# Linear and memory attention on one core: diagonal blocks of two query tiles packed into shared exponentials

## The chip, the cores and the metric

The kernel runs on one core of one Trainium2 chip. The time is the device time of one execution in microseconds; the runs of the kernel before gave 514.81, 516.71 and 517.5 us, median 516.71. A profiled execution is a run of its own, with a time of its own.

## What is computed

Two layers A (softmax attention in segments, with a memory) and two layers B (linear attention with learned features), in the order A, B, A, B, each with LayerNorm ahead and a residual. 2048 tokens, width 512, 32 heads of 16.

```python
# A, for each segment s of 512 tokens
logits = einsum('bhqd,bhkd->bhqk', qs, ks) * scale + mask     # causal inside the segment
a_dot = einsum('bhqk,bhkd->bhqd', softmax(logits), vs)
pq = phi(qs)                                   # phi(t) = t + 1 for t > 0, else exp(t)
a_mem = (pq @ M) / (pq @ z + 1e-06)            # state of the segments before
o = g * a_mem + (1.0 - g) * a_dot              # g = sigmoid(beta)
M = M + phi(ks)^T @ vs;  z = z + sum(phi(ks))
# B
phi_q = concat(softmax(q @ w_phi), softmax(-q @ w_phi));  phi_k likewise from k
o = (phi_q @ (phi_k^T @ v)) / (phi_q @ sum(phi_k) + 1e-06)
# around both: x = x + f(layernorm(x)) @ wo
```

## The kernel before

The residual stream X stays in SBUF for the whole run, 16 tiles of 128 tokens (a tile's tokens on the partitions, in order). A segment is 4 tiles. "Layer" below is one A with the B behind it; there are two.

**Order of the work.** Nothing is issued in program order. Each call to `P.add` records an operation with its reads, writes, a cost and the engines that may run it; `schedule` then simulates the engines with these costs and writes out one queue for each engine, in which the order is fixed. Among the operations that could start, the one with the lowest priority number goes first; the numbers are the tuple PLAN (L44, 3455 entries, one for each operation in order of recording; L296). An operation with two possible engines (`copy`, L784: ACT or DVE) is put where it starts first. A wait on the chip is a wait on semaphores of the operations that it depends on. Two strips of score matmuls that lie in different row groups are written out in turn, two matmuls of the one, two of the other (L689 to L695). Where PE would be idle, matmuls on zeros (L1450) are put in.

**A, segment by segment.** `ln` (L999): statistics on DVE, the power -0.5 on POOL, the normalised tile `xn` on DVE, transposed to `xnT` by DMA (SP's queue) or by PE for the tiles in `by_pe`. `a_proj` (L1057): for the keys either one token-major projection, split into even and odd heads and transposed by DMA, or, for tiles in `by_pe`, a feature-major projection with two masked evictions (L1076) *and* a token-major one (L1085) for phi. `by_pe` is all four tiles of segment 0 of both layers, and nothing else. `phi` (L1025): exponential on ACT, minimum with 1 on DVE, then max(t, 0) plus that on DVE. Then queries (QT), PhiQ, and V.

`a_att` (L1152) is the softmax attention of a group of query tiles ts; groups are (0, 1) and (2, 3) for segments 0 to 2, and (0, 1), (2), (3) for segment 3 (L1392). For every key tile j and parity of heads there is a strip part of 128 columns for each query tile i >= j, for four groups g of 8 heads. Four parts fill 512 columns; two banks of PSUM (two heads) make a tile `st` of 128 x 1024, written by row-tiled matmuls of 32 contraction rows. One ACT exponential of 1024 (L1199) evicts it to PT (12 buffers). A diagonal part (i = j) is computed in full, 128 keys by 128 queries, and its upper half is set to zero afterwards by POOL (L1203). With P transposed, `PT` is the stationary operand of the PV matmuls (17 columns: 16 values and the gated normaliser). DVE takes the reciprocal of the sums (L1222) and multiplies, one tile at a time (L1224); the memory part AM is added per tile (L1233). `a_out` (L1243) projects and adds to X on DVE (L1241).

**B.** `b_keys` (L1251): two exponentials a tile on ACT (L1261), sums (L1262) and reciprocals (L1264) on DVE, the scaling of 128 x 1024 on POOL (L1266; on DVE for the last two tiles of segment 3). `b_queries` (L1300) and `b_out` (L1337) follow when the keys of all four segments are in KV; the output goes out with `store` in layer 1. The B outputs of layer 0 lie mostly beside layer 1's attention; chunk 0 of them stands between the layers, since segment 0 of layer 1 needs it.

Of the kernel before, what the change touches and what calls it, by code (L numbers as in the profile page):

```python
# [26 lines left out]
ENGS = ("pe", "act", "dve", "pool", "sp")  # L27
HOP = dict(pe=0.03, act=0.03, dve=0.03, pool=0.05, sp=0.04)
# [11 lines left out]
OVERLAP = 0.14  # L40
PRI = dict(mem=-5.0, state=0.5, aout=-0.2, lnx0=-0.5, lnx1=-10.0, ap0=9.5, aps=4.625, bo0=-6.0, bo1=3.5, lnb=-7.5, bk=2.0, bks=2.2, kv=14.0, q00=58.0,
# [140 lines left out]
)  # L182


# [1311 lines left out]
```

## Time and profile before

| | |
|---|---|
| median of three runs | 516.71 us |
| profiled execution | 518.92 us |
| its span, first to last instruction | 517.3 us |
| granted PE clock, mean | 0.987 |
| busy: PE, ACT, DVE, POOL | 487.7, 440.3, 432.3, 269.8 us |
| exponentials of scores (L1199) | 320, 1054 ns each, 308.2 us busy |
| selections on diagonals (L1203) | 168 of 512, 80 of 256, 32 of 768 elements; 660, 419, 886 ns |
| normalising multiplies (L1224) | 128 of 128 elements, 281 ns |
| score matmuls | 832 of 256 columns, 896 of 128 |
| PV matmuls | 2560 of 17 columns |
| matmuls on zeros (L1450) | 125, 19.7 us |

In rows of the profile an engine, a line, what is written and read, the shape and the count come first, then busy time and mean length of one, then the idle time ahead of them and what ended it. Busy times overlap where an engine works on two instructions at once, so the distance from one start to the next is often shorter than the length of one. PEld is PE's loading of weights.

### The profile page before, as it was taken

Reading aid. Unit: us, or ns where it says so; the run is one execution under the profiler, and the core shown is the slowest. Engines: PE = TensorE matmul, PEld = TensorE weight load, DVE = VectorE, ACT = ScalarE, POOL = GpSimd, SP = SyncE. Lnnn points to the kernel's source line nnn. Section 1 sums busy time; section 2 is a strip of 40 time slices with the busy share of each in tenths; the row PEclk is TensorE's granted clock in tenths of the full one; section 3 lists DMA queues with packets and bytes.
Section 4 is the critical chain, followed back from the end, with each engine's and each line's share of the span. In section 5 each row is a group of like instructions: output and inputs, shape, how many; then the busy total and the mean of one; then the engine's idle time right before and its main releaser. Section 6 shows DMA issues by size and latency. Waiting matters only on the chain.

```text
span 517.3 us, 16946 instructions
## 1 busy us (share of the span) xinstructions
PE 487.7 (94%) x7194; PEld 306.4 (59%) x7286; DVE 432.3 (84%) x1025; ACT 440.3 (85%) x593; POOL 269.8 (52%) x396
## 2 busy tenths in 40 slices
PE   9989999999999999999999999999999999999997
PEld 6656455656456656656665555655555555565664
DVE  6998789968669888899968788988998677887995
ACT  3989999989999999854599999899999999974443
POOL 5464486635567766230147468456854476631234
PEclk9989999989999999999999999999999999997999
DMA  8956433332200411200115425224433121110034
GB/s 240 272 93 94 79 67 53 38 57 46 49 13 15 59 39 22 26 4 5 22 22 74 55 39 94 54 41 64 63 63 63 23 55 33 13 37 4 4 82 142
DMA packets 94538, 29.96 MB, mean 58 GB/s; under 512 B 86272, under 2 KB 94464, under 8 KB 94464
## 3 DMA queue, kind: packets, MB, share of 16 engines
q1 hardware_dynamic: 93216, 27.83, 30.0%
q10 hardware_dynamic: 1248, 1.06, 0.8%
q8 instruction: 57, 0.93, 0.8%
q14 instruction: 17, 0.14, 0.1%
HBM read 6.32 MB, written 2.10 MB: 16 GB/s over the span
## 4 chain that ended last, share of the span: by engine, by line
PE 52%; ACT 32%; DVE 11%; DMA 2%; issue 2%
PE PS L729 48%; ACT PT L1199 25%; PE PS L1450 3%; DMA xnT<-xn 2%; ACT Ek L1261 2%; ACT phi L1027 2%; DVE stats L1007 1%; PE PS L807 1%; DVE X L1241 1%; DVE O L1358 1%; DVE KV L1293 1%; DVE EQ L1332 1%; DVE Rkv L1295 1%; DVE rd L1357 0%; DVE PhiK L1029 0%
## 5 line engine op out<-in xcount | busy, mean ns | idle before, releaser
L1199 ACT ACTIVATE PT<-PS 128x1024 bf16<-128x1024 f32 x320 | 308.2, 1054 | 10.0 <-PE PS L729 9.1
L1203 POOL TENSOR_SCALAR_AFFINE_SELECT PT<-PT 128x512 bf16<-128x512 bf16 (+2 forms) x280 | 169.7, 617 | 131.7 <-ACT PT L1199 128.0
L729 PEld LDWEIGHTS PS<-VT,PT 128*128 128x128 bf16 x2560 | 78.1, 96 | 23.3 <-issue 5.8
L729 PE MATMUL PS<-VT,PT 128*128 128x17 bf16 x2560 | 85.7, 171 | 0.1
L729 PE MATMUL PS<-QT,KT 32*128 32x256 bf16 (+1 forms) x864 | 77.4, 245 | 4.5 <-ACT PT L1199 2.9
L1266 POOL TENSOR_TENSOR Ek<-Ek,rZ 128x1024 bf16<-128x1024 bf16 x28 | 55.3, 1977 | 44.7 <-DVE rZ L1264 44.7
L729 PE MATMUL PS<-QT,KTo 32*128 32x128 bf16 (+1 forms) x864 | 76.1, 243 | 2.4 <-ACT PT L1199 1.0
L729 PEld LDWEIGHTS PS<-QT,KT 32*128 32x128 bf16 x864 | 32.4, 92 | 39.2 <-ACT PT L1199 24.0
L1261 ACT ACTIVATE Ek<-PS 128x512 bf16<-128x512 f32 x64 | 35.8, 611 | 13.1 <-PE PS L729 12.8
L729 PEld LDWEIGHTS PS<-QT,KTo 32*128 32x128 bf16 x864 | 35.0, 93 | 19.6 <-ACT PT L1199 11.6
L1241 DVE TENSOR_TENSOR X<-X,PS 128x512 bf16<-128x512 bf16 x54 | 36.8, 682 | 11.3 <-PE PS L729 10.7
L1262 DVE TENSOR_REDUCE Zk<-Ek 128x64 f32<-128x1024 bf16 x32 | 38.6, 1212 | 8.2 <-ACT Ek L1261 7.9
L1007 DVE BATCH_NORM_STATS2 stats<-X 128x6 f32<-128x512 bf16 x64 | 43.3, 683 | 1.5 <-DMA X<-in_A_x_dram 0.8
L1013 POOL TENSOR_TENSOR rstd<-rstd,negh 128x2 f32<-128x2 f32 (+1 forms) x38 | 26.3, 694 | 33.3 <-DVE rstd L1011 32.1
L729 PE MATMUL PS<-xnT,WA_q 128*128 128x128 bf16 x512 | 35.9, 221 | 0.1
L729 PE MATMUL PS<-WA_v,xnT 128*128 128x512 bf16 x110 | 31.9, 380 | 2.4 <-issue 1.0
L729 PE MATMUL PS<-WA_k,xnT 128*128 128x512 bf16 x111 | 31.4, 380 | 2.8 <-issue 1.0
L729 PEld LDWEIGHTS PS<-xnT,WA_q 128*128 128x128 bf16 x512 | 29.6, 99 | 7.0 <-issue 2.8
L1224 DVE TENSOR_TENSOR O<-PS,r 128x128 bf16<-128x128 f32 x128 | 31.5, 281 | 1.2
L729 PE MATMUL PS<-WA_o,OT 128*128 128x512 bf16 x115 | 30.0, 380 | 1.4 <-issue 0.6
L729 PE MATMUL PS<-WB_o,OT 128*128 128x512 bf16 x118 | 29.6, 380 | 1.4 <-DVE QT L785 0.5
L1017 DVE TENSOR_SCALAR xn<-X,mv,rstd 128x512 bf16<-128x512 bf16 x64 | 26.9, 430 | 2.0 <-DMA xnT<-xn 0.9
(135 smaller groups left out, 839.1 us busy)
## 6 DMA issues: line engine op xcount, KB each, us to landing
out_dram<-X SPq DMA_DIRECT2D x16, 128.0 KB, 1.8
X<-in_A_x_dram SPq DMA_DIRECT2D x3, 512.0 KB, 10.0
EQ<-in_B_wqkv_dram SPq DMA_DIRECT2D x2, 512.0 KB, 10.5
OT<-O SPq DMA_TRANSPOSE x46, 2.5
xnT<-xn SPq DMA_TRANSPOSE x36, 2.5
WA_o<-in_A_wo_dram SPq DMA_DIRECT2D x1, 512.0 KB, 10.1
WB_v<-in_B_wqkv_dram SPq DMA_DIRECT2D x1, 512.0 KB, 12.3
WB_o<-in_B_wo_dram SPq DMA_DIRECT2D x1, 512.0 KB, 9.9
```

The costliest lines, as they stand in the source:

```text
L729: return e.matmul(o, l, r, start=st, stop=sp, tile_position=(basep(l), basep(o)))
L1007: self.dve(lambda e, t=t: e.bn_stats(self.stats[:, t, :], self.X[:, t, :]), 0.60, [R("X", t)], [R("stats", t)])
L1013: self.pool(lambda e, ve=ve, n=n: e.tensor_tensor(ve, ve, self.negh[:, 0:1].to_broadcast([128, n]), ALU.pow), 0.76, [R("rstd", t0 + i) for ...
L1017: self.dve(lambda e, t=t, xn=xn: e.tensor_scalar(xn.ap[:], self.X[:, t, :], self.mv[:, t, 0:1], self.rstd[:, t:t + 1], op0=ALU.subtract, o ...
L1199: self.act(lambda e, st=st, pt=pt: e.activation(pt.ap[:].rearrange("p b c -> p (b c)"), self.ps[:, st.slot[0] * 512:st.slot[0] * 512 + 102 ...
L1203: self.pool(lambda e, dv=dv, nd=nd: e.affine_select(dv(), dv(), [[0, 2], [0, nd], [1, 128]] if nd > 1 else [[0, 2], [1, 128]], ALU.is_ge, 0.0,
L1224: self.dve(lambda e, r1=r1, view=view, c=c, g=g: e.tensor_tensor(o[c].ap[:, g, :].rearrange("p (h d) -> p h d", d=DH), view()[:, c, :, 0:1 ...
L1241: self.dve(lambda e: e.tensor_tensor(X[:, t, :], X[:, t, :], self.bank(gen), ALU.add), 0.61, [R("X", t), gen()], [R("X", t)])
L1261: self.act(lambda e, sgn=sgn, Ek=Ek, gen=gen: e.activation(Ek.ap[:, sgn, :], self.bank(gen), ACT.Exp, scale=1.0 - 2.0 * sgn), 512, [gen()] ...
L1262: self.dve(lambda e, Ek=Ek, Zk=Zk: e.tensor_reduce(Zk.ap[:], Ek.ap[:].rearrange("p s (h j) -> p s h j", h=H), AX.X, ALU.add), 1.15, [Ek(0) ...
L1266: scale = lambda e, Ek=Ek, rZ=rZ: e.tensor_tensor(Ek.ap[:].rearrange("p s (h j) -> p (s h) j", j=DH), Ek.ap[:].rearrange("p s (h j) -> p ( ...
L1450: ins = e.matmul(self.ps[:, b * 512:b * 512 + 256], self.warm[:, 0:128], self.warm[:], start=True, stop=True)
```

## The change

**X with halves exchanged.** In odd tiles, tokens 64 to 127 lie on partitions 0 to 63 and tokens 0 to 63 on partitions 64 to 127, from the load to the store. Each odd tile is loaded and stored in two halves; the loads of segments 1 to 3 become four each.

**Diagonal blocks.** A diagonal block of 128 x 128 has three quarters of 64 x 64 that are not all zero. For a pair of tiles (i0, i1), the early quarter of i0 (its first 64 keys and queries) lies on partitions 0 to 63, that of i1 on partitions 64 to 127, since its halves are exchanged. Both go into one strip: the early quarters of all 32 heads and both tiles are two tiles `ta` (kept in PT) with two exponentials for the pair, 32 matmuls of 64 columns each. The rest, for each group g and each y of two, is 64 late queries of i0, 128 of i1 against the keys of i0, and 64 late queries of i1: 256 columns a head, one exponential of 1024 into the middle of a tile `DT` (384 columns a head). Three POOL selections of 256 elements (one of them from `ta` into DT, one on 64 partitions) and one DVE minimum with a mask `late` (from `ta` into DT) fill in the triangles. Blocks off the diagonal are as before. PT has 7 buffers, DT 4.

**Pairs throughout.** Segment 3 has the groups (0, 1) and (2, 3) as well. Normalising is one multiply for both tiles, the memory add one of 1024 (DVE or POOL).

**First phi of keys.** For the tiles in `by_pe` of segment 0, phi is taken from the feature-major keys and transposed to PhiK by DMA; the token-major projection goes.

**Smaller edits.** The residual of segment 3 of A and of B's chunk 0 in layer 0 is added by an identity matmul, and X comes back by a copy (ACT or DVE); the key scaling of B on POOL is two instructions of 512; the minimum in phi, `xn` (not in `by_pe`) and Rkv may go to POOL.

**Order.** PLAN has 3539 entries, all new, and ON fixes the engine of 209 operations that could run on two (68 ACT, 120 DVE, 21 POOL). The rest of `schedule` does the same as before (the added branch needs PAIR > 0).

```diff
+PAIR = 0.0
...
 PLAN = (
...
+ON = {
+    "act": (
...
     def schedule(self):
         ops = self.ops
+        for e, some in ON.items():
+            for i in some:
+                ops[i].eng = (e,)
...
-        self.p_PT = slots("PT", 12, [128, 2, 512], BF16)
+        self.p_PT = slots("PT", 7, [128, 2, 512], BF16)
+        self.p_DT = slots("DT", 4, [128, 2, 2, 384], BF16)
...
-            load("act" if t % 2 == 0 else "sp", self.X[:, t, :], xv[t * 128:(t + 1) * 128, :], [R("X", t)], 0.4)
+            eng = "act" if t % 2 == 0 else "sp"
+            if t % 2:
+                for h in range(2):
+                    load(eng, self.X[64 * h:64 * h + 64, t, :], xv[t * 128 + 64 * (1 - h):t * 128 + 64 * (1 - h) + 64, :], [R("X", t)], 0.15)
...
+            flat = s <= 2 and tt in by_pe
+            if flat:
+                fm = lambda a: a[:].rearrange("p (g c) -> p g c", g=NG)
+                self.phi(t2, lambda t2=t2: fm(t2.ap), lambda gen=gen: self.bank(gen).rearrange("p (g c) -> p g c", g=NG), gen, t2(), shape=fm)
+                self.transposed(lambda tt=tt: seg["PhiK"].ap[:, tt, :].rearrange("p (a c) -> p a c", a=4), lambda t2=t2: t2.ap[:], [t2()], [seg["PhiK"](tt)], False, pre=[seg["PhiK"]])
...
+        full = [[(0, j), (1, j)] for j in range(i0)]
...
+        ta = [self.p_PT.tile() for _ in range(2)]
+        kr = [K(j) for K in K2 for j in ts] + [QT(i % 2) for i in ts]
+        for y in range(2):
...
+            st = strips(y, ta[y], lambda st, y=y: [x for g in range(NG) for par in range(2) for h in range(2) for b in range(2) for x in [
+                mm(st, b, (2 * g + par) * 64, K2[par], 2 * y + b, g, ts[h] * 128 + 64 * h, 64, 192 * h, 64, p=64 * h)]], kr)
+            self.act(lambda e, st=st, pt=ta[y]: e.activation(
+                pt.ap[:].rearrange("p b c -> p (b c)"), self.ps[:, st.slot[0] * 512:st.slot[0] * 512 + 1024], ACT.Exp, scale=0.25), 1024, [st()], [ta[y]()])
...
+                st = strips(y, dt, lambda st, y=y, g=g: [x for par in range(2) for b in range(2) for x in [
+                    mm(st, b, par * 256, K2[par], 2 * y + b, g, i0 * 128, 128, 64, 192)]] + [x for par in range(2) for b in range(2) for x in [
+                    mm(st, b, par * 256 + 192, K2[par], 2 * y + b, g, i1 * 128, 128, 128, 64)]], kr)
+                self.act(lambda e, st=st, dt=dt: e.activation(
+                    dt.ap[:, :, :, 64:320], self.ps[:, st.slot[0] * 512:st.slot[0] * 512 + 1024].rearrange("p (b u c) -> p b u c", b=2, u=2), ACT.Exp, scale=0.25), 1024,
+                    [st()], [dt("m")])
...
+                select(0, 0, src=early)
+                P.add(("dve",), lambda e, early=early, block=block: e.tensor_tensor(block(320), early(), self.late[:, None, None, :].to_broadcast([128, 2, 2, 64]), ALU.min),
+                      {"dve": 0.2}, [ta[y](), R("late")], [dt(("x", 320))], lat=0.09, port=True)
+                select(64, 64)
+                select(256, 0, 64)
...
+        added = s == 3
...
+        if added:
+            mms.append((lambda: (self.bank(gen), self.ident[:], self.X[:, t, :], False, True), 512))
...
-                self.pool(scale, 1.9, [rZ(), Ek(0), Ek(1)], [Ek(0), Ek(1)])
+                for sgn in range(2):
+                    self.pool(lambda e, Ek=Ek, rZ=rZ, sgn=sgn: e.tensor_tensor(Ek.ap[:, sgn, :].rearrange("p (h j) -> p h j", j=DH), Ek.ap[:, sgn, :].rearrange("p (h j) -> p h j", j=DH),
+                                                        rZ.ap[:, sgn, :, None].to_broadcast([128, H, DH]), ALU.mult), 1.0, [rZ(), Ek(sgn)], [Ek(sgn)])
...
-        PAIRS, LAST = ((0, 1), (2, 3)), ((0, 1), (2,), (3,))
+        PAIRS, LAST = ((0, 1), (2, 3)), (((0, 1), (2, 3)))
...
-                self.b_out(0, *prev[0], nb - 12, nb - 10, False, by_pe=range(4))
+                self.b_out(0, *prev[0], nb - 12, nb - 10, False, by_pe=range(4), add_pe=range(4))
```

More of the change, by code (lines that the diff above doesn't have):

```diff
@@ L435, in grant, with second @@
             return at, got
+        def second(op):
+            at = 0.0
+            for t in list(op.pre) + op.tiles:
+                if t.slot is not None:
+                    continue
+                p = t.pool
+                if isinstance(p, Pool):
+                    f = [tile_free(h) for h in p.holder]
+                    f = sorted(x for x in f if x is not None)
+                    if len(f) < 2:
+                        return None
+                    at = max(at, f[1])
+                else:
+                    f = [tile_free(h) for h in p.holder]
+                    best = None
+                    for skip in range(2):
+                        got = None
+                        for banks in p.kinds[t.kind]:
+                            if best is not None and set(banks) & set(best[1]):
+                                continue
+                            x = [f[b] for b in banks]
+                            if None not in x and (got is None or max(x) < got[0] - 1e-9):
+                                got = (max(x), banks)
+                        if got is None:
+                            return None
+                        best = got
+                    at = max(at, best[0])
+            return at
         ready = {e: set() for e in ENGS}
@@ L449, in schedule @@
         n_ops = len(ops)
+        now = 0.0
+        strict = PAIR > 0
         def commit(i, e, t, g):
@@ L491, in schedule @@
             choice = None
+            if PAIR > 0:
+                behind = free["act"] + sum(ops[x].cost["act"] for x in sorted(ready["act"]) if ops[x].eng == ("act",))
             for e in ENGS:
@@ L502, in schedule @@
                         at = max(at, held[other[e]] - OVERLAP)
+                    if op.rows and PAIR > 0:
+                        s2 = second(op)
+                        r2 = [ops[x].ready for x in ready[e] if ops[x].rows and ops[x].rows != op.rows]
+                        tm = max(at, s2, min(r2)) if s2 is not None and r2 else None
+                        if tm is not None and behind >= tm + AHEAD:
+                            at = tm
+                        elif (tm is None or tm > at + HOLD) and strict and behind > max(at, now) + PAIR:
+                            continue
                     cand.append((at, op.pri, i, g))
@@ L513, in schedule @@
                     choice = (c, e)
+            if choice is None and strict:
+                strict = False
+                continue
+            strict = PAIR > 0
             if choice is None:
@@ L518, in schedule @@
             op = ops[i]
+            now = max(now, t)
             if e == "pe" and self.idle:
@@ L1227, in a_att, with strips, mm @@
-        outs = []
-        P.pri = p1 + PRI["add"] * (p1 - p0) / n_units
+        i0, i1 = ts
+        nt = 2
+        full = [[(0, j), (1, j)] for j in range(i0)]
+        n_quads = NG * (len(full) + 1) + 1
+        o2 = self.p_O2.tile()
+        def strips(y, kind, write, reads):
+            st = self.PS.tile("st")
+            mms = write(st)
+            self.pe([(f, n * 32) for f, n in mms], reads, [st()], pre=[kind], lat=0.14, cost=0.23, rows=y + 1)
+            return st
+        def mm(st, b, c, K, a, g, k0, kn, q0, qn, p=0):
+            return (lambda: (self.ps[p:p + kn, st.slot[b] * 512 + c:st.slot[b] * 512 + c + qn], K.ap[32 * a:32 * a + 32, g, k0:k0 + kn],
+                             QT.ap[32 * a:32 * a + 32, g, q0:q0 + qn], True, True)), qn
@@ L1244, in a_out @@
         self.P.tag = (self.L, "aout%d" % s)
+        R = self.R
         gen = self.gen()
-        self.pe([(lambda g=g, gen=gen: (self.bank(gen), oT.ap[:, g, :], self.WA["o"][:, g, :], g == 0, g == 3), 512) for g in range(NG)],
-                [oT(), self.R("WA", "o")], [gen()])
-        self.residual(s * 4 + i, gen, self.X)
+        t = s * 4 + i
+        added = s == 3
+        mms = [(lambda g=g, gen=gen: (self.bank(gen), oT.ap[:, g, :], self.WA["o"][:, g, :], g == 0, g == 3 and not added), 512) for g in range(NG)]
+        if added:
+            mms.append((lambda: (self.bank(gen), self.ident[:], self.X[:, t, :], False, True), 512))
+        self.pe(mms, [oT(), R("WA", "o")] + ([R("ident"), R("X", t)] if added else []), [gen()])
+        if added:
+            self.copy(lambda: self.X[:, t, :], lambda: self.bank(gen), 512, [gen()], [R("X", t)])
+        else:
+            self.residual(t, gen, self.X)
     def b_keys(self, c, xnT, pris, pri1):
@@ L1429, in build @@
                 grp = PAIRS if s < 3 else LAST
[L1430 removed]
+                xb = self.ln(s, [ends[g[-1]] + PRI["lnb"] for g in grp], grp, by_pe=(2, 3) if s == 3 else (), pool=self.p_EQ if s < 2 else None, gap=s == 3)
                 self.b_keys(s, xb, [ends[g[-1]] + PRI["bk"] + PRI["bks"] * n for g in grp for n in range(len(g))], ends[3] + PRI["kv"])
```

228 lines of the change are left out of this document (124 added, 104 removed), and 285 rows, old and new, of tables (ON, PLAN).

## The prediction

> **What bounds the kernel now.** I read the busy shares of the page first, then the stages, then the waits, then single rows. The stages are cut where the first exponential of the scores starts (17.5 us) and the last ends (216 us), and the same in layer 1 (262 and 460 us):
>
> ```profile
> core 0: us, PE busy (x) PEld busy (x) DVE busy (x) ACT busy (x) POOL busy (x), PEclk, DMA share, GB/s
> 0.00:17.50 17.50, 16.21 (x149) 12.01 (x152) 12.53 (x50) 7.49 (x13) 7.12 (x19) 1.00 0.89 269
> 17.50:216.00 198.50, 186.52 (x3019) 116.62 (x3058) 165.92 (x384) 190.68 (x244) 119.74 (x179) 0.98 0.37 58
> 216.00:262.00 46.00, 44.67 (x506) 29.52 (x508) 42.52 (x98) 25.49 (x46) 6.68 (x7) 1.00 0.05 10
> 262.00:460.00 198.00, 188.53 (x2981) 115.34 (x3019) 166.01 (x393) 189.92 (x244) 119.61 (x178) 1.00 0.31 50
> 460.00:517.00 57.00, 51.79 (x550) 32.90 (x555) 45.28 (x102) 26.69 (x47) 16.70 (x14) 0.94 0.22 58
> ```
>
> The two attention stretches are 396.5 of 517.3 us. In them ACT is busy 96%, DVE 84%, POOL 60%, PE 94 to 95%. PE's share has to be checked, since ends of matmuls are modelled. Four 512-column matmuls in a row take
>
> ```profile
> 102.80 1.03 PE L729 MATMUL PS<-WA_o,OT 128*128 128x512 bf16 x4
> ```
>
> so (1.03 - 0.38) / 3 = 0.217 us from one to the next, against a mean length of 0.380 in the groups: PE's busy time counts the end of a matmul again under the next. The waits of layer 1's stretch say who is early:
>
> ```profile
> PEld PS L729 <- ACT PT L1199: 22.1, 58, 1.1
> ...
> ACT PT L1199 <- PE PS L729: 5.3, 12, 1.0
> ```
>
> PE's weight loads wait 22.1 us for exponentials, the exponentials 5.3 us for PE. So **ACT sets the pace of both stretches**, with DVE next; between and behind them (103 us) ACT is under 56% busy, and DVE and PE are the busy ones (92 and 97% in 216 to 262).
>
> **The exponentials (the term that decides).** Rows:
>
> ```profile
> 99.42 4.67 ACT L1199 ACTIVATE PT<-PS 128x1024 bf16<-128x1024 f32 x5
> ...
> L1199 ACT ACTIVATE PT<-PS 128x1024 bf16<-128x1024 f32 x320 | 308.2, 1054 | 10.0 <-PE PS L729 9.1
> ```
>
> Five take 4.67 us with 1.05 us for the last, so one costs ACT (4.67 - 1.05) / 4 = 0.905 us. Before, a segment needs 40 of them (12 + 28). After, a pair at tiles 0 and 1 needs 2 (the early quarters of all heads) + 4 x 2 = 10, a pair at 2 and 3 needs 2 + 4 x (4 + 2) = 26: 36. That is 4 x 8 = 32 fewer, 16 a layer: **14.5 us of ACT's time per stretch**.
>
> **What DVE gets.** 128 new minima of 128x256 bf16, 64 a stretch. No such row exists; the nearest with two SBUF inputs is below it, with its mean of 524 ns:
>
> ```profile
> L1233 DVE TENSOR_TENSOR O<-O,AM 128x512 bf16<-128x512 bf16 x24 | 12.3, 524 | 0.2
> L1356 DVE TENSOR_TENSOR rd<-PS,ze 128x32 f32<-128x32 f32 x32 | 5.5, 174 | 1.3 <-PE PS L729 1.1
> ...
> 73.10 0.49 DVE L1224 TENSOR_TENSOR O<-PS,r 128x128 bf16<-128x128 f32 x2
> ```
>
> Bounds per minimum: 0.09 us (the 32-wide one, 0.174 less some 0.08 of overlap with the next) and 0.44 (the 512-wide one, less the same). I take 0.20, near the 128-wide pace below: 12.8 us a stretch. The normalisation goes from 64 multiplies of 128 (0.49 - 0.28 = 0.21 apart, 13.4 us) to 32 of 256 (between 0.21 and 0.60, the pace of the 512-wide residual; taken 0.34, 10.9 us): -2.5. Six adds of 1024 for twelve of 512, fewer reciprocals: -1. The residual of segment 3 goes to an identity matmul and a copy that ACT or DVE can take; with the phi minima, xn and Rkv that POOL may now take: 0 to -5. Net about +7: 173 of DVE time where there were 166.
>
> **What POOL gets.** Instead of 280 selections, 384 of 256 elements. The row is there:
>
> ```profile
> L1203 POOL TENSOR_SCALAR_AFFINE_SELECT PT<-PT 128x512 bf16<-128x512 bf16 x168 | 110.4, 660 | 116.2 <-ACT PT L1199 115.1
> L1203 POOL TENSOR_SCALAR_AFFINE_SELECT PT<-PT 128x256 bf16<-128x256 bf16 x80 | 33.1, 419 | 10.1 <-ACT PT L1199 7.8
> ```
>
> 384 x 0.419 = 161 us for 172. Two halves of the key scaling for one of 1.98 us: the same sum within 0.1 us each. POOL stays near 60%; nothing. The chain from an exponential to its PV grows from 0.66 to 2 x 0.42 us, which a fourth DT buffer covers; without that cover it is 0.2 us for each of 64 groups.
>
> **What PE gets.** A pair of score strips of 16 matmuls:
>
> ```profile
> 210.19 0.23 PE L729 MATMUL PS<-QT,KT 32*128 32x128 bf16 x4
> 210.26 0.22 PE L729 MATMUL PS<-QT,KTo 32*128 32x128 bf16 x4
> 210.31 0.22 PE L729 MATMUL PS<-QT,KT 32*128 32x128 bf16 x4
> 210.37 0.22 PE L729 MATMUL PS<-QT,KTo 32*128 32x128 bf16 x4
> 210.52 0.60 PE L729 MATMUL PS<-xnT,WB_q 128*128 128x512 bf16 x2
> ```
>
> 0.33 us, plus some 0.10 to enter (the next strip starts 0.31 us behind a 512-column matmul of 0.217). 160 pairs become 144: -7 us. In 16 of these, 64 matmuls of 64 columns stand in for 16: sixteen fours, each between 0.027 (half of a 128-column four) and 0.06 us, so 0.6 to 1.1 us a pair; taken 0.9: +9. The DT strips move the same columns as before. The identity adds are 12 x 0.217 = +2.6, the dropped token-major keys of the two first segments 32 x 0.217 = -6.9. PE: about -2 us; no change of the bound.
>
> These 64-column matmuls write 64 output partitions each, two stacked; before has none of that form. The Trainium skill (TensorEngine Tiling (Array Packing), Tile-to-Partition Mapping, its restrictions) says that tiling the columns in this way switches fast weight loading off; no run so far shows it. By that rule the time would go from the sum below towards that of the last rival.
>
> **What a stretch is worth.** If ACT kept its 96%, (190.7 - 14.5) / 0.96 = 183.5: -15 us. If DVE became the bound with the 92% that it reaches in 216 to 262, 173 / 0.92 = 188: -10.5. Both will be near, so I take **-12.5 each, -25 in all**.
>
> **The ends of the layers.** Segment 3 treated tile 2 alone and tile 3 alone; now both end together. What stood beside tile 3's 16 exponentials falls behind the last one: tile 2's output, LayerNorm and B keys, on DVE 0.61 + 0.12 + 0.32 + 1.13 + 0.46 + 1.13 = 3.8 us. In layer 0, DVE gives up five residuals there (5 x 0.60 = 3.0) to the half idle ACT, and PE 16 x 0.217 = 3.5: 0 (-3 to +3). In layer 1 it gives up one: **+3** (0 to 5).
>
> **Start, transposes, stores.** Sixteen key matmuls less before the first scores (-3.5 at most), but the first strip now needs the keys of two tiles (two evictions of 0.70 us more): 0. The 8 new DMA transposes of PhiK (2.5 us to landing in the DMA rows) feed a state that the next segment uses, tens of us later; if that cover were gone, 2.5 us each. More issues on SP's queue (loads +11, stores +8): SP does nothing else, transposes apart; at the end one more issue, under 0.5 us.
>
> **Sum.** Against the profiled execution's 518.9 us (span 517.3): -25 + 0 + 3 = -22, 496.9. The median of the runs is 516.7, 2.2 below the profiled one; by that, **495 us**.
>
> **Rivals.**
> *ACT's gain comes through whole*, and the forced choices move copies of the middle stage to the idle ACT: -15 x 2, -3 in the middle, 0 in the tail: 518.9 - 33 - 2.2 = 483.5. For it: DVE has 16% idle, POOL 40%. Against: DVE at 94%.
> *DVE becomes the bound.* Each minimum 0.44 us because POOL selects at the same time: 64 x 0.24 = 15 more, 188 / 0.96 = 196: -2.5 each, less what goes to POOL (5 / 0.96): -7.5 each: 518.9 - 15 + 3 - 2.2 = 505. For it: the same 512-wide xn takes 0.32 to 0.54 us in one group, with POOL busy beside it. The Trainium skill (GPSIMD Engine Reference, Specifications) says that POOL and VectorE share SBUF interfaces and contend when a VectorE instruction has two SBUF inputs, as these minima have; L1233's mean over its fastest records agrees.
> *Buffers.* PT goes from 12 to 7: two hold the early quarters for a whole pair, four a group, one is left. If ACT waits half an exponential (0.45 us) at each of 32 groups of a stretch: +14.5, nothing is won there: 518.9 + 3 - 2.2 = about 517 with the tail, 512 if the waits hide other ACT work. Does the order fit the program? Counted by hand, the operations go from 3455 to 3539, and the two lists have these lengths, so each operation has a place; that the change doesn't take hold is not to be expected.
> *Slower: weights of the early quarters load one by one.* 64 loads at the row's 92 ns are 5.9 us a pair instead of 0.33; 8 pairs a stretch, +44 us on PE ahead of each pair's exponentials. Half of it hidden: +22 a stretch, 518.9 + 44 - 22 - 2.2 = 539. It decides from 22 / 16 = 1.4 us over 0.33, 1.7 us a pair. Against: the fours above run side by side.
>
> **Chances.** Forecast 0.50 (488 to 500), whole gain 0.20, DVE bound 0.14, buffers 0.09, slower 0.07. Range 480 to 513: it leaves out the slower case, half of the buffers' case and a little below 480. Within 0.5% (2.6 us, about what a measurement of this kernel can tell) half of the buffers' case and some of DVE's: 0.07. Faster 0.85, slower 0.08.
>
> **What would show it.** Right: 288 exponentials, stretches near 186 us, ACT and DVE both over 90%. DVE bound: minima over 0.35 us and exponentials waiting for PE that waits for DVE. Buffers: strips waiting for PV. Column strips: 64 small matmuls taking over 1.7 us. Wrong altogether, if the stretches shrink by 15 and the stages behind them grow by as much.

## The result, and the profile after

The changed kernel takes **556.22 us** (median of 4 runs, 553.04 to 558.98) where the kernel before takes 516.39 in the runs beside it: a ratio of 1.077 (95% interval 1.071 to 1.084). The forecast was 495, range 480 to 513: the kernel was to gain 22 us and lost 40. Where a run of a kernel lies more than 1.5% over its fastest, only the faster ones are compared; of e5_late_f32 below this leaves one. The profiled execution took 558.98 us, its span 557.3, at a mean clock of 0.947 against 0.987.

The same view as in the prediction, busy time of each engine by stage, cut where the first exponential of the scores starts and the last one ends:

```profile
core 0: us, PE busy (x) PEld busy (x) DVE busy (x) ACT busy (x) POOL busy (x), PEclk, DMA share, GB/s
0.00:24.70 24.70, 20.57 (x262) 16.87 (x265) 13.84 (x45) 8.88 (x15) 7.63 (x22) 1.00 1.02 241
24.70:229.60 204.90, 183.94 (x3322) 121.70 (x3360) 166.99 (x375) 181.73 (x236) 142.41 (x256) 0.95 0.33 53
229.60:271.50 41.90, 40.97 (x500) 26.72 (x503) 38.44 (x87) 25.17 (x48) 7.95 (x10) 1.00 0.06 12
271.50:493.80 222.30, 203.46 (x3456) 129.41 (x3494) 177.93 (x401) 187.08 (x246) 149.17 (x259) 0.92 0.30 47
493.80:557.30 63.50, 53.81 (x549) 35.28 (x556) 47.54 (x99) 24.59 (x46) 17.16 (x17) 0.96 0.23 51
```

Read the second column against that of before (17.5, 198.5, 46, 198, 57). The cut of before at 460 us is too early: its last exponential starts at 462.7 and ends at 463.7 us. So I compare by the starts of the first and the last exponential of each layer. The start is 7 us longer (17.5 to 24.7), the middle 5 shorter (47.9 to 42.9), the tail 10 longer (54.6 to 64.5), and the attention stretches, which were to shrink by 12.5 each, grow by 7 and 21. In them ACT is busy 89% and 84%, not 96%; POOL's busy time is up by 52 us, DVE's by 13; the PE clock is 0.95 and 0.92.

The next rows are groups of instructions (busy time, mean ns of one, then idle time ahead of them and what ended it):

```profile
L1311 ACT ACTIVATE DT<-PS 128x1024 bf16<-128x1024 f32 x128 | 129.9, 1037 | 21.1 <-PE PS L806 20.5
L1301 ACT ACTIVATE PT<-PS 128x1024 bf16<-128x1024 f32 x128 | 129.4, 1038 | 15.6 <-PE PS L806 14.8
...
L1321 DVE TENSOR_TENSOR DT<-PT,late 128x256 bf16<-128x256 bf16 x128 | 46.8, 376 | 5.1 <-PE PS L806 3.4 <-ACT PT L1290 1.6
...
L1114 POOL TENSOR_SCALAR xn<-X,mv,rstd 128x512 bf16<-128x512 bf16 x19 | 41.1, 2161 | 1.4 <-DMA EQ<-xn 0.8
...
L1133 POOL TENSOR_SCALAR phi<-phi 128x512 bf16<-128x512 bf16 x12 | 18.0, 1502 | 2.1 <-ACT phi L1131 1.4
```

With 32 more in the early strips there are 288 exponentials, as counted. But ACT now waits some 41 us for PE ahead of them (9 before), and POOL runs two kinds of instruction that it did not run before: 19 normalisations of 2.16 us and 12 minima of 1.50 us. The code gives both a cost of 0.66 us; on DVE the same two last 0.50 and 0.37.

One stall shows how the pieces hang together (the timeline of the changed kernel; in brackets how long the engine had been idle and what ended it):

```profile
340.78 2.21 POOL L1114 TENSOR_SCALAR xn<-X,mv,rstd 128x512 bf16<-128x512 bf16 x1
...
343.38 2.09 POOL L1114 TENSOR_SCALAR xn<-X,mv,rstd 128x512 bf16<-128x512 bf16 x1
...
345.55 1.50 POOL L1133 TENSOR_SCALAR phi<-phi 128x512 bf16<-128x512 bf16 x1
...
347.08 0.69 DVE L1135 SCALAR_TENSOR_TENSOR PhiK<-PS,phi 128x512 bf16<-128x512 f32 x1 [3.56 <-POOL phi L1133]
...
350.38 1.02 ACT L1311 ACTIVATE DT<-PS 128x1024 bf16<-128x1024 f32 x1 [4.34 <-PE PS L806]
```

POOL's phi is late, DVE stands still for 3.6 us, PE (behind DVE) has nothing to do for 2.7 us, ACT waits 4.3 us for PE, and from 349.7 to 354.4 the matmuls go at half their usual pace (two of 512 columns take 1.01 us there and 0.60 at 355.6). I call the sum of such stretches the **half-speed time**: 17 us before (5.5 of it at the start), 55 after. It is read from the lengths of matmuls and good to some us; the mean granted clocks, 0.987 and 0.947, make 14 and 59 us at half speed, without the start.

### The profile page after: what moved, and what is told of

Read it like the earlier page. It is cut to its first block, busy times and chain, and to the rows that moved or that the text cites. A ratio compares the mean times of both kernels' runs of the same rounds, so it can differ in the third digit from the quotient of the medians.

```text
span 557.3 us, 18921 instructions
## 1 busy us (share of the span) xinstructions
PE 502.7 (90%) x8076; PEld 330.0 (59%) x8170; DVE 444.7 (80%) x1003; ACT 427.4 (77%) x585; POOL 324.3 (58%) x563
## 3 DMA queue, kind: packets, MB, share of 16 engines
q8 instruction: 64, 1.05, 0.8%
## 4 chain that ended last, share of the span: by engine, by line
PE 45%; DVE 20%; POOL 12%; ACT 11%; DMA 5%; SPq 3%; issue 3%; DVEq 0%; POOLq 0%
PE PS L806 43%; POOL DT L1317 4%; ACT PT L1301 3%; SPq L870 3%; POOL xn L1114 3%; ACT DT L1311 3%; DVE stats L1099 3%; DMA OT<-O 3%; POOL phi L1133 2%; DVE DT L1321 2%; DMA X<-in_A_x_dram 2%; DVE X L1364 2%; DVE PhiQ L1135 2%; POOL Ek L1403 1%; ACT Ek L1392 1%
## 5 line engine op out<-in xcount | busy, mean ns | idle before, releaser
L1311 ACT ACTIVATE DT<-PS 128x1024 bf16<-128x1024 f32 x128 | 129.9, 1037 | 21.1 <-PE PS L806 20.5
L1301 ACT ACTIVATE PT<-PS 128x1024 bf16<-128x1024 f32 x128 | 129.4, 1038 | 15.6 <-PE PS L806 14.8
L1317 POOL TENSOR_SCALAR_AFFINE_SELECT DT<-DT 64x256 bf16<-64x256 bf16 (+1 forms) x256 | 107.7, 441 | 41.1 <-ACT DT L1311 40.2
L1317 POOL TENSOR_SCALAR_AFFINE_SELECT DT<-PT 128x256 bf16<-128x256 bf16 x128 | 56.8, 452 | 67.7 <-PE PS L806 46.6
L806 PE MATMUL PS<-QT,KT 32*64 32x64 bf16 (+3 forms) x1280 | 83.3, 229 | 9.7 <-ACT DT L1311 4.3
L806 PE MATMUL PS<-VT,DT 128*128 128x17 bf16 x1536 | 80.6, 171 | 5.9 <-DVE PhiK L1135 2.7
L806 PEld LDWEIGHTS PS<-VT,DT 128*128 128x128 bf16 x1536 | 72.1, 97 | 15.5 <-issue 2.9
L1403 POOL TENSOR_TENSOR Ek<-Ek,rZ 128x512 bf16<-128x512 bf16 x56 | 58.0, 1054 | 32.8 <-DVE rZ L1395 32.7
L806 PE MATMUL PS<-QT,KTo 32*64 32x64 bf16 (+3 forms) x1280 | 75.8, 225 | 0.0
L1321 DVE TENSOR_TENSOR DT<-PT,late 128x256 bf16<-128x256 bf16 x128 | 46.8, 376 | 5.1 <-PE PS L806 3.4
```

Source lines behind the costliest of these rows:

```text
L806: return e.matmul(o, l, r, start=st, stop=sp, tile_position=(basep(l), basep(o)))
L1301: self.act(lambda e, st=st, pt=pt: e.activation(pt.ap[:].rearrange("p b c -> p (b c)"), self.ps[:, st.slot[0] * 512:st.slot[0] * 512 + 102 ...
L1311: self.act(lambda e, st=st, dt=dt: e.activation(dt.ap[:, :, :, 64:320], self.ps[:, st.slot[0] * 512:st.slot[0] * 512 + 1024].rearrange("p ...
L1317: lambda e, c=c, src=src, base=base, p=p, block=block: e.affine_select(block(c, p), src() if src else block(c, p), [[0, 2], [0, 2], [1, 64 ...
L1321: P.add(("dve",), lambda e, early=early, block=block: e.tensor_tensor(block(320), early(), self.late[:, None, None, :].to_broadcast([128, ...
L1403: self.pool(lambda e, Ek=Ek, rZ=rZ, sgn=sgn: e.tensor_tensor(Ek.ap[:, sgn, :].rearrange("p (h j) -> p h j", j=DH), Ek.ap[:, sgn, :].rearra ...
```

## The experiments

The edits are given in words. Unless it says otherwise, a kernel keeps the order of every queue of the kernel that it is made from, so that only the instructions named differ. Each time stands beside runs of the kernel before on the same chip, whose medians lay between 516.06 and 517.29 us.

### POOL's long instructions, and the loads

```diff
-  POOL: xn = (X - mean) * rstd;  phi = min(phi, 1)
+  POOL: a selection of 512 elements that copies            # e1_short_pool, 31 instructions
...
-  a tile's second half load waits for its first half
+  it doesn't                                               # e2_no_load_wait; e3_both has both edits
...
-  xn, phi minimum: DVE or POOL
+  DVE                                                      # e4_dve, the order worked out anew
```

> The order of all queues stays that of after; only POOL's 19 xn and 12 minima are replaced by a selection that copies the 512 elements (left out: the normalisation of these 19 tiles and these 12 minima), about 0.66 us each instead of 2.16 and 1.50. Theory 1 (these 31 instructions hold POOL's queue, and selections, transposes and PSUM wait behind them): 30 to 40 us come back, 516 to 527, and the granted clock rises to 0.97 or more. Theory 2 (the packing itself, its buffers and selections, costs the time): at most the queue's own 38 us shrink unnoticed, time stays over 545.

> The order of all queues stays that of after; only the wait of an X load's second half for the landing of the first half is gone (what reads X waits for both). Theory 3 (this wait blocks SP's queue at the start and costs the 7 us by which the first exponential is late): first exponential at 18 to 20 us, 548 to 551. Theory 2: first exponential earlier, but the time the same within 2 us since later waits take it back.

> Both edits. If theories 1 and 3 are separate causes, their gains add: 508 to 520, at or near before. If the packing costs the time, over 540.

> All xn and all minima of phi on DVE, computed in full; the order is worked out anew from the same list of priorities. Theory 1: 525 to 540, better than after, since no long instruction stands in POOL's queue, but with the order no longer the one that the list was made for. Theory 2: 545 to 560.

Measured: 542.51 (ratio 1.050, 1.035 to 1.064), 556.22, 542.22 and 569.38 us. POOL's 31 instructions cost 14 us, and the loads' wait nothing that can be told: the first exponential comes at 23.0 instead of 24.7 us, and that is lost later. So the long POOL forms are a third of the loss and not the whole of it; theory 1 had them at 30 to 40 us. With all of them on DVE the kernel is slower still (1.102), but there the order differs too, so this run doesn't price the move.

### DVE's new minima

In e1_short_pool the largest single stall is this (timeline):

```profile
317.26 1.05 POOL L1407 TENSOR_TENSOR Ek<-Ek,rZ 128x512 bf16<-128x512 bf16 x1
...
317.91 4.52 DVE L1325 TENSOR_TENSOR DT<-PT,late 128x256 bf16<-128x256 bf16 x1
318.27 1.52 POOL L1321 TENSOR_SCALAR_AFFINE_SELECT DT<-PT 128x256 bf16<-128x256 bf16 x4
319.75 0.78 POOL L1321 TENSOR_SCALAR_AFFINE_SELECT DT<-DT 64x256 bf16<-64x256 bf16 x2
320.50 1.04 POOL L1407 TENSOR_TENSOR Ek<-Ek,rZ 128x512 bf16<-128x512 bf16 x1
321.51 1.56 POOL L1321 TENSOR_SCALAR_AFFINE_SELECT DT<-DT 64x256 bf16<-64x256 bf16 x4
...
322.82 0.39 PE L806 MATMUL PS<-xnT,WA_q 128*128 128x128 bf16 x2 [4.16 <-DVE O L1351]
```

A minimum that takes some 0.28 us when POOL is idle lasts 4.52 us, as long as POOL runs one instruction behind the other, and PE stands still for 4.16 us. Five edits ask what holds it:

```diff
-  DT = min(PT, late)            # late in 16 bits
+  late in 32 bits               # e5_late_f32; e6_short_late: the same in e1_short_pool
+  DT = max over an axis of 1    # e9_reduce: one input; from e1_short_pool
+  DT = 0.5 (memset)             # e8_memset: no input; from e1_short_pool
...
+  e7_all: e6_short_late, no wait between half loads, one PhiK transpose earlier in SP's queue
```

> Only the mask of DVE's 128 new minima is kept in 32 bits instead of 16; the order of every engine is the same. In the profile of the changed kernel three minima last 1.0 to 2.0 us while POOL's selections run without a pause beside them, and in the run with short POOL work one lasts 4.5 us, for a normal 0.26. Theory 'held': a minimum in its 16-bit form is held up by a POOL that does not pause; in the mixed form the long ones go (none over 0.8 us, each 0.33 to 0.40 instead of 0.26 to 0.38) and the time falls by 5 to 12 us from 556, to 544 to 551. Rival 'two inputs from SBUF are enough': long minima stay, time 553 to 559. Rival 'only longer': minima of 0.35 us on a loaded DVE, no gain from the long ones, 556 to 562.

> As the run with short POOL work (POOL's 19 normalisations and 12 minima of phi left out in favour of selections of 0.65 us that copy), and DVE's new minima with the mask in 32 bits. Order unchanged. In the run with short POOL work the half-speed stretches of the PE clock at 322, 418 and 455 us each follow a minimum of 1.5 to 4.5 us. Theory 'held': those three go with it, 542 minus 4 to 15 us: 527 to 538. Rivals as in the run before: 540 to 546.

> As the run before (19 normalisations and 12 minima of phi on POOL left out in favour of copying selections), and besides: the second half of a token tile's load doesn't wait for the first, and one DMA transpose of the keys' phi stands ahead of four transposes of weights in SP's queue, which it waited behind in all runs so far (ACT then waits 2.3 to 3.3 us for its buffer at 33 us and the PE clock is at half speed from 38 to 48). Theory 'single stalls, each followed by a slow clock': the wait at 33 us and the slow clock at 38 to 48 go, 4 to 8 us less than the run before: 521 to 532. Rival 'the loss is spread over the whole stretch': within 2 us of the run before.

> As the run with short POOL work (19 normalisations and 12 minima of phi on POOL left out), and DVE's 128 new minima replaced by a reduction over an axis of one element, which has one input from SBUF and no mask (the mask of the early tile is left out). It should last about 0.4 us like the minima with a 32-bit mask, whose run took 549. Of all DVE forms before and after, reductions and reciprocals show no long ones beside POOL. Theory 'held': none over 0.6 us, and 6 to 15 us under the run with a 32-bit mask: 534 to 543. Rival 'only length': 546 to 552.

> As the run with short POOL work (POOL's 19 normalisations and 12 minima of phi left out in favour of copying selections; 542 us), and DVE's 128 new minima replaced by memsets of the same 256 elements, which read nothing: the early query tile's last block is left out. Order unchanged. Theory 'held': without inputs from SBUF no write of these is held up by POOL, so 12 to 19 us of DVE's excess and the PE stalls behind it go: 518 to 532. Rival 'DVE's share is only length': 128 x 0.1 us shorter, by the 4 to 7 us that 128 x 0.13 us cost in the two runs with a 32-bit mask: 536 to 540. Rival 'POOL and DVE are not on the way any more': 540 to 545.

Measured: 556.24 (one run), 549.27 (1.063, 1.049 to 1.078), 551.07, 541.55 (1.048, 1.039 to 1.057) and 535.53 us (1.036, 1.025 to 1.048). With a 32-bit mask the minimum takes 0.42 us, and long ones remain (up to 1.1, 2.1 and, in e7_all, 4.6 us): the rival "two inputs from SBUF are enough" is right, my theory of the 16-bit form is not. The reduction has one input and is as long as the 32-bit minimum, and not one of 128 is over 0.42 us (mean 0.40); it is 8 us faster than e6_short_late (the intervals overlap), but only 1 us faster than e1_short_pool. So it is the second input of the minimum, not its length, that POOL can hold up. But in that run the hold passes to the next instruction that can be held: at the same place a minimum of phi lasts 3.87 us.

```profile
L1325 DVE TENSOR_REDUCE DT<-PT 128x256 bf16<-128x256 bf16 x128 | 49.7, 399 | 3.5 <-ACT PT L1294 1.7 <-PE PS L806 1.6
...
317.57 3.87 DVE L1135 TENSOR_SCALAR phi<-phi 128x512 bf16<-128x512 bf16 x1
```

The Trainium skill (SBUF — State Buffer, SBUF: two separate sides) says that VectorE and GpSimd share one pair of ports by an exclusive lock, which a DVE instruction in a mode of two ports or with two SBUF inputs also takes, and that the other waits for the end of the instruction that has it. The held minima and the free reductions agree; the length doesn't: here DVE waited through a row of POOL instructions (4.5 us), not for one of at most 1.05 us.

With memsets (mean 0.27 us, as a minimum alone) the time falls by 1.4% or 7 us against e1_short_pool; the intervals of the two overlap. The theory 'held' had 518 to 532; 535.5 lies beside the rival 'DVE's share is only length' (536 to 540). So that the minima cost time by being held is not shown. The transpose of PhiK ahead in SP's queue did what it should (ACT's wait of 2 us for it is gone) and the time did not move: e7_all against e6_short_late. A stall that goes was no gain here.

### The packing without a fitted order

```diff
-PLAN = (3, 4, 5, ...)
+PLAN = ()                      # n_b from the kernel before
+PLAN = (), no ON, xn and minima of phi on DVE    # n_a1 from the changed kernel
```

> The changed kernel without its list of priorities and without its forced choices of engines; normalisation and minima of phi on DVE alone, as in the kernel before. All of the computation is done. With a sister run of the kernel before without its list this shows the packing by itself, in an order that is fitted to neither. Theory 'the packing itself gains, the fitted order loses it': 10 to 25 us under the sister run. Theory 'the packing brings nothing because ACT is not the only pace': within 8 us of it. No forecast of its absolute time but 540 to 600.

> The kernel before without its list of priorities (all of the computation is done); its sister, the changed kernel without list and forced engines and with normalisation and minima of phi on DVE, took 595. Theory 'the packing itself gains, the fitted order loses it': 605 to 620. Theory 'ACT is not the only pace, the packing brings nothing': 587 to 603. Theory 'the packing's own instructions cost (held minima, longer chain of selections, fewer buffers, slow PE clock behind the stalls), whatever the order': 550 to 586.

Measured: n_a1 595.13 (591.22 to 599.05), n_b 568.84 us (568.47 to 569.21). Without any fitted list, and without POOL's long forms, the change as a whole costs 26 us; n_b lies where the third theory had it (550 to 586). So the loss is not one of this list alone. It is one other order only: both kernels fall back on the same constants in the code, and whether these suit the kernel before better is not shown.

### What a stall costs

```diff
+  DVE: a reduction of 2000 copies of a constant, once in each segment     # b_stall, from the kernel before
```

> The kernel before in its own order, with one extra DVE instruction of about 2.1 us (a reduction of 2000 copies of a constant into a spare column) ahead of one normalisation in each of the 8 segments: 17 us of DVE time, like minima held up by POOL. Theory 'a stall is followed by a slow PE clock': the time grows by more than is put in, 18 to 35 us, and the half-speed PE time grows from 17 us to 35 and over. Rival 'a stall is passed on as it is': 10 to 17 us, half-speed time near 17. Rival 'absorbed', since DVE is busy 84%: under 8 us.

Measured: 545.93 us (1.056, 1.047 to 1.066), 29 us more, where the eight instructions last 2.2 us each, 17.8 together. The half-speed time grows from 17 to 57 us. The first row below is the granted clock of b_stall in 40 slices of the span (tenths of full speed, 9 is 90% or more), the second that of the changed kernel:

```profile
PEclk9987999999997979999998799699997999998999
```

```profile
PEclk9986899999998999999989979799999798789999
```

Behind six of the eight stalls PE runs at half speed for 6 to 10 us. Behind two it does not: PE stands still until 93.6 us for 1.7 us and until 471.7 us for 1.1 us, and the granted clock stays at 1.00 for 20 us behind both (93 to 115 and 471 to 494 us). So a wait of this length can bring the slow clock and need not. On the sum the theory holds, 1.6 us for each us put in.

### What ACT's time is worth

This is the step on which the forecast rested, so it is tried in the kernel before itself.

```diff
-  exp over 1024 columns
+  exp over 912 columns, but in the first segment           # b_exp: before; a_exp: changed kernel
```

> The kernel before in its own order; 280 of its 320 exponentials (all but those of the first segment) leave out the last 112 of 1024 columns: 280 x 112 x 0.83 ns = 26 us of ACT's time, about what the packing takes from it. Nothing else changes. Theory of the prediction 'ACT sets the pace of both stretches': 19 to 27 us less, 490 to 498. Rival 'ACT is one of several in a chain, its time counts by a half at most': 503 to 512. Rival 'not on the path': 513 to 518.

> The changed kernel in its own order; 252 of its 288 exponentials leave out 112 of 1024 columns: 23.5 us of ACT's time. Nothing else changes. In it ACT is busy 84 to 89% of the stretches, against 96% before. Theory 'in the changed kernel ACT no longer sets the pace': 0 to 8 us less, 548 to 556. Rival 'it still does': 14 to 24 us less, 532 to 542.

Measured: b_exp 509.40 us (0.986, 0.979 to 0.993), **8 us less for 26 us of ACT's time**; a_exp 555.88, nothing for 23.5 us. The chain that ended last (the work followed back from the last instruction, at each step to what released it) had ACT at 32% before and at 8% in b_exp:

```profile
PE 52%; ACT 32%; DVE 11%; DMA 2%; issue 2%
...
PE 66%; DVE 18%; ACT 8%; DMA 5%; POOL 1%; issue 1%; ACTq 0%; DVEq 0%
```

and ACT's waits ahead of exponentials grow from 9 to 16 us, while PE's weight loads wait less for exponentials (before, then b_exp):

```profile
PEld PS L729 <- ACT PT L1199: 39.4, 101, 1.1
...
ACT PT L1199 <- PE PS L729: 9.1, 19, 1.1
...
PEld PS L729 <- ACT PT L1200: 28.0, 69, 1.0
...
ACT PT L1200 <- PE PS L729: 16.4, 33, 1.5
```

So part of the wait changes sides: PE is the next, close behind. Is PE then the pace?

```diff
-  for dt in range(4): matmul of 512 columns (keys, values, queries of B)
+  for dt in range(3)                                       # b_pe; b_both: with b_exp's edit as well
```

> The kernel before in its own order; 96 of its 512-column matmuls (a quarter of the inner dimension in the key, value and query projections of the second kind of layer) are left out: 96 x 0.217 = 21 us of PE's time, three quarters of it or so in the attention stretches. Theory 'PE sets the pace': 496 to 505. Theory 'ACT and PE are both close to the limit, so either alone gives a third of its time': 507 to 513. Rival 'PE has room, as the prediction read it': 514 to 518.

> Both cuts in the kernel before, in its own order: 112 of 1024 columns of 280 exponentials (26 us of ACT) and 96 matmuls (21 us of PE) left out. The cut of the exponentials alone gave 509. Theory 'ACT and PE take turns, what one gives the other takes': more than the sum of the single gains, 485 to 499. Rival 'DVE and the order are next': the sum of the single gains or less, 500 to 508.

Measured: b_pe 514.47 (0.996, 0.992 to 0.999), 2 us for 21 us of PE; b_both 507.15 us (0.980, 0.974 to 0.986), 9.4 us for 47, the sum of the two. The chain of b_both has DVE at 32% (16% in b_pe). The time is that of the rival "DVE and the order are next": in this fixed order of five queues neither ACT nor PE sets the pace alone, nor both together, although ACT is busy 96% and PE 94%. That DVE or the order does is argued: DVE was not shortened in the kernel before, and ACT's time was not tried in an order worked out anew.

### Selections, and the slow clock

```diff
-  POOL: selections of 256 elements;  DVE: minima
+  selections of 64 elements but in the first segment; memsets               # e10_sel, from e8_memset
+  behind every second group of PV matmuls one matmul of 240 columns on zeros  # e11_warm, from e10_sel
```

> As the run with memsets for minima (535.5 us; it leaves out POOL's 19 normalisations, 12 minima of phi and DVE's 128 minima), and POOL's 384 selections work on 64 of their 256 elements but for the first segment: some 0.24 instead of 0.45 us each, 70 us less on POOL. The masks of the diagonal blocks are mostly left out. Theory 'the longer chain of selections takes the rest': 516 to 527. Rival 'POOL is off the path once its long forms are gone': 531 to 538.

> As the run with short selections (532.6 us; it leaves out POOL's 19 normalisations and 12 minima of phi, DVE's 128 minima, and three quarters of most selections), and behind every second of the 256 groups of matmuls of 17 columns one more matmul of 240 columns into an unused part of the same bank: 128 x 0.10 = 13 us more for PE. Order unchanged. Theory 'the slow clock comes from too little streaming': half-speed time falls from 46 us to under 25, which pays for the added work: 520 to 533. Rival 'the slow clock follows from waits': half-speed time 40 or more and 538 to 548.

Measured: e10_sel 532.58 us (1.030, 1.022 to 1.038), 3 us under e8_memset, which can't be told from none: POOL is off the path once its long forms are gone. The long DVE instructions beside it are gone too (no phi minimum over 0.68 us). Its half-speed time is still 46 us. One such stretch begins at 425 us (timeline of PE in e10_sel):

```profile
419.74 0.61 PE L806 MATMUL PS<-xnT,WA_q 128*128 128x128 bf16 x8
420.19 0.45 PE L806 MATMUL PS<-VT,DT 128*128 128x17 bf16 x12
...
422.95 0.20 PE L806 MATMUL PS<-VT,PT 128*128 128x17 bf16 x2
423.00 0.20 PE L806 MATMUL PS<-VT,DT 128*128 128x17 bf16 x2
...
425.15 1.01 PE L806 MATMUL PS<-xnT,WA_q 128*128 128x128 bf16 x8
```

Eight matmuls of 128 columns take 0.61 us at 419.7 and 1.01 at 425.2, and between them PE was never idle for more than 0.3 us (by the modelled ends of matmuls); it ran mostly matmuls of 17 and 64 columns. With 128 added matmuls of 240 columns (13 us of work) the stretch at 425 is gone, the half-speed time is 25.5 us, the clock 0.977 instead of 0.958, and the time is 533.59 us, the same: the added work pays for itself. Both figures just miss what the theory of too little streaming had (under 25 us, 520 to 533). It fits that stretch; the stretches at 39 and 445 us stay. The first row is the clock of e10_sel, the second that of e11_warm:

```profile
PEclk9986999999999999999999989999998957899999
```

```profile
PEclk9987999999999999999999999999999997899999
```

## Why the prediction was wrong, point by point

Forecast and measured time lie 61 us apart. Some 21 of these are gain that did not come: the sum had 25 us for ACT's time, and at the rate measured in b_exp it is 4. The other 40 are costs that the sum had at nothing or too low.

**"ACT sets the pace of both stretches" (failed, the step on which the gain rested).** I read it from ACT's 96% and from who waits for whom, and turned ACT's time into time almost one to one: 29 us into 25. In the kernel's own order 26 us of ACT are worth 8 (b_exp), 0.30 us for each; in the changed kernel 23.5 are worth nothing (a_exp). The waits that I showed (22 us of PE behind ACT, 5 us of ACT behind PE) say who comes last, not by how much; the next one stood a fraction of a microsecond behind. My doubt about PE's 94% was beside the point: PE alone isn't the pace either (b_pe).

**"32 fewer exponentials give ACT 14.5 us a stretch" (failed in the sum).** The count is right, but ACT's busy time in the two stretches falls by 11.8 us only (380.6 to 368.8), in part since 24 more evictions of some 0.5 us stand on it (100 copies instead of 72 at the helper's line, 4 masked ones fewer), in part since exponentials that wait overlap less: 1.01 us of busy time for each instead of 0.96, where I had counted 0.905. I had named the forced choices, and credited them to DVE, not charged them to ACT. At b_exp's 0.30 these 11.8 us are 4.

**DVE, "+7 a stretch" (right in the sum, by errors that cancel).** DVE is up 13.0 us in both. The minimum lasts 0.38 us on the mean; the 18 that meet no POOL instruction last 0.28, about what I took (0.20 and the overlap), the others 0.39. What went to ACT and POOL makes up for it. The rival "DVE becomes the bound" had the hold as a price of 0.24 us for each; over 0.28 us it is 13 us in all, 4 of them in the four minima of 0.8 to 2.0 us, the rest in small pieces. What this cost the kernel is open: memsets gave 7 us, not clear of noise, and the reduction, which isn't held, 1.

**POOL, "nothing" (failed).** The selections are as forecast (169 us, forecast 161), but I took the option "xn and phi may go to POOL" as a relief of DVE and priced it on POOL at nothing, without a row for either form. 31 instructions, 59 us of POOL, 14 us of the time (e1_short_pool): of the costs, the one that is shown.

**PE, "-2" (right for the strips, wrong for the sum).** PE's busy time rises by 15 us (487.7 to 502.7). The early strips, my rival on the slow side, are cheap. The timeline of a strip of 32 matmuls:

```profile
280.99 0.22 PE L806 MATMUL PS<-QT,KT 32*64 32x64 bf16 x4
281.04 0.20 PE L806 MATMUL PS<-QT,KTo 32*64 32x64 bf16 x4
...
281.37 0.31 PE L806 MATMUL PS<-VT,DT 128*128 128x17 bf16 x6
```

0.38 us to the next instruction, a pair in 0.64 (at 23.9 us), for my 0.9 and a threshold of 1.7. By the Trainium skill's rule (TensorEngine Tiling (Array Packing), Tile-to-Partition Mapping) that column tiling loses fast weight loading, the loss would have come from here; by these rows it didn't.

**Start, "0" (failed, +7.2).** The text said that SP does nothing else. The two halves of an odd tile are written one behind the other, a wait of the second half holds everything behind it in SP's queue (an issue of 3.56 us at 9.69), and the order that follows puts tile 1's statistics behind the first phi:

```profile
9.69 3.56 SPq L870 DMA_DIRECT2D X<-in_A_x_dram  x1
```

```profile
15.46 0.69 DVE L1099 BATCH_NORM_STATS2 stats<-X 128x6 f32<-128x512 bf16 x1 [1.58 <-DMA X<-in_A_x_dram]
```

Before, all four statistics of the first segment had run by 7.5 us. The wait alone is worth 1.7 us of the first exponential (e2_no_load_wait); the rest is put down to the order, without a run of its own.

**Middle and tail, "0 and +3" (right in the sum, by luck).** They are -5.0 and +9.9, each outside the bounds given (-3 to +3, 0 to 5); together +4.9.

**The transposes of PhiK, "2.5 us each if the cover were gone" (right, in one place).** The cover was named wrongly: not the state waits for them but the two buffers of phi, for 2 to 3 us at 33 us.

**The buffers, a rival.** Its sign was strips waiting for PV. All 45 waits of ACT ahead of exponentials in the changed kernel ended with a score matmul, none with a PV matmul that frees a buffer. But strips and PV stand in one queue, where the place of a strip behind PV would not show as a wait, so this stays open.

**Slips in the prediction.** The buffers' rival adds up to 519.7 us (518.9 + 3 - 2.2), not 517, and the whole gain to 483.7, not 483.5; the cut at 460 us is 3.7 us ahead of the end of the last exponential. The forecast rests on none of these.

**What was not in the sum: the clock.** Half-speed time 17 to 55 us. Matmuls go at half their pace there, so 38 us more are up to 19 us of PE. In the runs it followed stalls (six of eight in b_stall) and, in one place, poor streaming (e11_warm). What it costs by itself is not shown: in e11_warm 20 us of it went, 13 us of matmuls came, and the time stayed.

**What is settled.** Of the 40 us, 14 are POOL's long forms; about 7 went with DVE's minima and about 3 with the selections, neither told from 0. The 16 that e10_sel still lacks go with 6.4 us of later start (23.9 against 17.5) and some 29 us more of half-speed time; that these two are all of it is argued, not shown. More waiting of PE it is not, as far as the records tell: in the changed kernel PE is not busy for 55 of 557 us, in the kernel before for 30 of 517 (some 90 matmul records are missing in both), but in e10_sel for 23 of 531. Open: whether seven PT buffers instead of twelve cost anything (there was no room to give them back, and another number changes the order), and whether a list fitted to POOL's measured costs would bring the changed kernel under the kernel before; neither was tried. No version of the changed kernel here is faster than the kernel before.

## What to carry to other kernels

Before a gain on the busiest engine is counted, shorten that engine's instructions in the kernel as it stands and see what the time does; in this kernel, with its queues in a fixed order, an engine busy 96% gave 0.30 us for each us. Price every engine that an operation may now run on by a row of that form on that engine, and if there is none, take the bound that hurts. Charge a stall with the slow clock that may follow on PE (here 1.6 us for each us of DVE put in), and look for instructions on one engine that can be held up by a busy neighbour.

## What the runs showed of the hardware that was not expected

- A DVE instruction with two SBUF inputs, and a 16-bit minimum with a constant from SBUF to SBUF, can stand still beside POOL through several POOL instructions: 0.28 us became 4.52, 0.29 became 3.87. A reduction with one input (128 of them, none over 0.42 us) and a memset (128 of 0.27 us) are not held.
- POOL's forms differ far more than their sizes: 512 elements a partition in 2.16 us with two per-partition scalars, 1.50 with a constant, 0.65 as a selection.
- The clock of PE can halve after waits much shorter than the slow stretch that follows. In b_stall PE had stood still for 0.8 to 2.1 us ahead of six half-speed stretches of 6 to 10 us, and waits of 1.7 and 1.1 us brought none; in e10_sel one stretch came without a wait over 0.3 us. The Trainium skill (TensorE: Matmul & The Clock Gate, Why this matters for your kernels) asks for no idle gaps over some 3 us; by these rows that is not enough.
